# Strassen's algorithm with seven products for the two FFN matrix products behind a linear-attention block

## The chip, the core and the metric

The kernel runs on one core of a Trainium2 chip. The metric is the device time of one execution in microseconds (us). PE is TensorE (matrix products), PEld its weight loads, DVE is VectorE, ACT is ScalarE, POOL is GpSimd, and SP is the queue that starts transfers. SBUF is the on-chip memory and PSUM holds the matrix products' sums. The kernel before takes 1322.14 us, the median of 3 runs (1321.06 to 1322.49).

## The reference

The attention has no softmax: k times v per head, q times that, a division by the root mean square over the 64 columns of a head, and a gain. Its 4,608 by 512 result goes through a gated feed-forward network (FFN). All of it is fp32; the three FFN weights come as 64-bit floats.

```python
kv = np.einsum('bhsd,bhse->bhde', k, v)              # batch 8, heads 8, seq 576, head_dim 64
o = np.einsum('bhsd,bhde->bhse', q, kv)
x = o / np.sqrt(np.mean(o * o, axis=-1, keepdims=True) + 1e-06) * g_norm
x = x.transpose(0, 2, 1, 3).reshape(4608, 512)
g = x @ w_gate                                       # 512 x 1536
val = x @ w_val                                      # 512 x 1536
out = g / (1 + np.exp(-g)) * val @ w_out             # 1536 x 512
```

## The kernel before

The 4,608 tokens are handled in nine blocks of 512. For each block the FFN has 12 "up" units (128 of the 1,536 gate and value columns each) and 4 "down" units (128 tokens each). The attention of the next block is cut into ten steps that stand between these units, so that TensorE never waits for it. Every weight piece is rounded on the chip from 64-bit words to fp32, on VectorE and ScalarE, during block 0.

```python
    class Words:
        def round_to(self, dst):                     # one piece, 128 x 512
            nc.scalar.activation(out=unit, in_=low, func=ACT.Copy, scale=2.0**-51, bias=2.0)
            nc.scalar.activation(out=mag.bitcast(F32), in_=high.bitcast(F32), func=ACT.Abs)
            nc.vector.tensor_scalar(out=mag..., op0=OP.max, op1=OP.min)
            nc.vector.tensor_scalar(out=sign, in0=high, ..., op0=OP.bitwise_and)
            nc.vector.scalar_tensor_tensor(out=mag, in0=mag, scalar=3, in1=sign, ...)
            nc.vector.tensor_tensor(out=dst.bitcast(U32), in0=mag..., in1=unit..., op=OP.add)

    # ... attention: kv, turn_q, product, rms, scale ...

    class Ffn:
        def up(self, j):
            g = g_psum.tile([P, BLK], F32, name="g")
            u = v_psum.tile([P, BLK], F32, name="u")
            for ps, w in ((g, wg), (u, wv)):
                for s in range(NS):                  # 4 steps of 128 along d_model
                    nc.tensor.matmul(ps, lhsT=w[:, s, P * j : P * (j + 1)], rhs=self.x[:, s, :], ...)
            silu = silu_pool.tile([P, BLK], F32, name="silu")
            nc.scalar.activation(out=silu, in_=g, func=ACT.Silu)
            nc.vector.tensor_tensor(out=self.h[:, j, :], in0=silu, in1=u, op=OP.mult)

        def down(self, t):
            ps = o_psum.tile([P, DM], F32, name="ops")
            for j in range(NF):                      # 12 steps of 128 along d_ff
                nc.tensor.matmul(ps, lhsT=self.h[:, j, P * t : P * (t + 1)], rhs=wo[:, j, :], ...)
            nc.scalar.copy(out=o, in_=ps)
            # ... store ...

    pieces = [("g", 0), ("v", 0), ("g", 1), ("v", 1)]
    for j in range(NF):
        pieces += [("g", j + 2), ("v", j + 2)] if j + 2 < NF else []
        pieces += [("o", j)]
```

Of the kernel before, what the change touches and what calls it, by code (L numbers as in the profile page):

```python
# [14 lines left out]
P = 128  # L15
# [3 lines left out]
def kernel(  # L19
# [17 lines left out]



    nc = tc.nc  # L40

    B, H, S, D = q.shape
# [1 line left out]
    FF = moe_w_gate.shape[1]  # L44
    T = 4
    BLK = P * T
    NB = NT // BLK
    NS = DM // P
    NF = FF // P
    KP = 96  # L50
    KT = S // KP
    eps = 1e-6
    assert NT == B * S and NT == NB * BLK and NB == B + 1 and S - BLK == BLK // B
    assert 2 * D == P and H == 2 * NS and KP * KT == S

    def pool(name, bufs, **kw):
        return ctx.enter_context(tc.tile_pool(name=name, bufs=bufs, **kw))

    consts = pool("consts", 1)
    ld_pool = pool("ld", 10)  # L60
    cv_pool = pool("cv", 2)
    qt_pool = pool("qt", 1)
    sq_pool = pool("sq", NS)
    st_pool = pool("st", 1)
    x_pool = pool("x", 2)
    h_pool = pool("h", 1)
    silu_pool = pool("silu", 2)
    o_pool = pool("o", 2)

    PS = bass.MemoryType.PSUM  # L70
    g_psum = pool("g_psum", 2, space=PS)
    v_psum = pool("v_psum", 2, space=PS)
    o_psum = pool("o_psum", 2, space=PS)
    a_psum = pool("a_psum", 2, space=PS)

    ident = consts.tile([P, P], F32, name="ident")
    make_identity(nc, ident)
# [16 lines left out]
    wg = consts.tile([P, NS, FF], F32, name="wg")  # L94
    wv = consts.tile([P, NS, FF], F32, name="wv")
    wo = consts.tile([P, NF, DM], F32, name="wo")

    class Words:

# [17 lines left out]
        def round_to(self, dst):  # L117
            halves = self.raw.rearrange("p (f w) -> p f w", w=2)
            low, high = halves[:, :, 0], halves[:, :, 1]

            unit = cv_pool.tile([P, BLK], F32, name="unit")
            nc.scalar.activation(out=unit, in_=low, func=ACT.Copy, scale=2.0**-51, bias=2.0)  # L122
            mag = cv_pool.tile([P, BLK], U32, name="mag")
            nc.scalar.activation(out=mag.bitcast(F32), in_=high.bitcast(F32), func=ACT.Abs)  # L124
            nc.vector.tensor_scalar(  # L125
                out=mag.bitcast(F32), in0=mag.bitcast(F32), scalar1=self.LOW, scalar2=self.HIGH,
                op0=OP.max, op1=OP.min,
            )
            sign = cv_pool.tile([P, BLK], U32, name="sign")
            nc.vector.tensor_scalar(out=sign, in0=high, scalar1=0x80000000, scalar2=None, op0=OP.bitwise_and)  # L130
            nc.vector.scalar_tensor_tensor(  # L131
                out=mag, in0=mag, scalar=3, in1=sign, op0=OP.logical_shift_left, op1=OP.bitwise_xor
            )
            a, b = self.shape[0], BLK // self.shape[0]
            nc.vector.tensor_tensor(  # L135
                out=dst.bitcast(U32),
                in0=mag.rearrange("p (a b) -> p a b", a=a, b=b),
                in1=unit.bitcast(U32).rearrange("p (a b) -> p a b", a=a, b=b),
                op=OP.add,
            )  # L140
# [14 lines left out]

    def round_w(name, j):
        dst = wviews[name][0]
        words.pop((name, j)).round_to(dst[:, j : j + 1, :] if name == "o" else dst[:, :, P * j : P * (j + 1)])

    class Att:  # L160

# [29 lines left out]
        def kv(self, js):  # L191
            if self.n == B:
                return
            if js[0] == 0:
                self.kv_ps = a_psum.tile([P, NS, D], F32, name="a")
            for j in js:
                for u in range(2):
                    rows = slice(u * D, (u + 1) * D)
                    for c in range(KT):
                        nc.tensor.matmul(  # L200
                            self.kv_ps[rows, j, :], lhsT=self.k[j][:, u, c, :], rhs=self.v[j][:, u, c, :],
                            start=(c == 0), stop=(c == KT - 1),
                        )
            if js[-1] == NS - 1:
                dst, ps = kvs[self.n % 3], self.kv_ps
                nc.scalar.copy(out=dst[0:D, :, 0:D], in_=ps[0:D])
                nc.vector.tensor_copy(out=dst[D:P, :, D:P], in_=ps[D:P])

        def turn_q(self, js):
            if js[0] == 0:  # L210
                self.qt = qt_pool.tile([P, NS, T, P], F32, name="qt")
            for j in js:
                ps = a_psum.tile([P, T, P], F32, name="a")
                hs = slice(2 * (j % 2), 2 * (j % 2) + 2)
                for t in range(T):
                    nc.tensor.transpose(ps[:, t, :], self.q[j // 2][:, t, hs, :], ident)  # L216
                nc.vector.tensor_copy(out=self.qt[:, j], in_=ps)

        def product(self, js):
            n, cut = self.n, self.cut  # L220
            if js[0] == 0:
                self.x = x_pool.tile([P, NS, BLK], F32, name="x")
                self.sq = []
            for j in js:
                ps = a_psum.tile([P, T, P], F32, name="a")
                for b, p0, p1 in ((n - 1, 0, cut), (n, cut, P)):
                    if p1 > p0:
                        nc.tensor.matmul(  # L228
# [4 lines left out]
                sq = sq_pool.tile([P, BLK], F32, name="sq")  # L233
                nc.scalar.activation(out=sq, in_=ps, func=ACT.Square)  # L234
                nc.vector.tensor_copy(out=self.x[:, j, :], in_=ps)  # L235
                self.sq.append(sq)

        def rms(self):


            ps = a_psum.tile([P, BLK], F32, name="a")
            for j in range(NS):
                nc.tensor.matmul(  # L243
                    ps[0:H, :], lhsT=head_of[:, j, :], rhs=self.sq[j], start=(j == 0), stop=(j == NS - 1)
                )
            z = st_pool.tile([H, BLK], F32, name="z")
            nc.vector.tensor_scalar(
                out=z, in0=ps[0:H, :], scalar1=1.0 / D, scalar2=eps, op0=OP.mult, op1=OP.add
            )
            y = st_pool.tile([H, BLK], F32, name="y")  # L250
            nc.vector.tensor_scalar(
# [9 lines left out]

        def scale(self, js):
            for j in js:
                ps = a_psum.tile([P, BLK], F32, name="a")
                nc.tensor.matmul(ps, lhsT=gain[:, j, :], rhs=self.y, start=True, stop=True)  # L265
                nc.vector.tensor_tensor(out=self.x[:, j, :], in0=self.x[:, j, :], in1=ps, op=OP.mult)  # L266

        def steps(self):
            lo, hi = (0, 1), (2, 3)
            return [  # L270
                lambda: self.kv(lo), lambda: self.kv(hi), lambda: self.turn_q(lo), lambda: self.turn_q(hi),
                lambda: self.product(lo), lambda: self.product(hi), self.rms, lambda: None,
                lambda: self.scale(lo), lambda: self.scale(hi),
            ]

    class Ffn:
        def __init__(self, n, x):
            self.n, self.x = n, x
            self.h = h_pool.tile([P, NF, BLK], F32, name="h")

        def up(self, j):
            g = g_psum.tile([P, BLK], F32, name="g")
            u = v_psum.tile([P, BLK], F32, name="u")
            for ps, w in ((g, wg), (u, wv)):
                for s in range(NS):
                    nc.tensor.matmul(  # L286
                        ps, lhsT=w[:, s, P * j : P * (j + 1)], rhs=self.x[:, s, :],
                        start=(s == 0), stop=(s == NS - 1),
                    )
            silu = silu_pool.tile([P, BLK], F32, name="silu")  # L290
            nc.scalar.activation(out=silu, in_=g, func=ACT.Silu)  # L291
            nc.vector.tensor_tensor(out=self.h[:, j, :], in0=silu, in1=u, op=OP.mult)  # L292

        def down(self, t):
            ps = o_psum.tile([P, DM], F32, name="ops")
            for j in range(NF):
                nc.tensor.matmul(  # L297
                    ps, lhsT=self.h[:, j, P * t : P * (t + 1)], rhs=wo[:, j, :],
                    start=(j == 0), stop=(j == NF - 1),
                )  # L300
            o = o_pool.tile([P, DM], F32, name="o")
            nc.scalar.copy(out=o, in_=ps)  # L302
            rows = out[BLK * self.n : BLK * (self.n + 1), :].rearrange("(p t) d -> p t d", t=T)
            nc.sync.dma_start(out=rows[:, t, :], in_=o)


    pieces = [("g", 0), ("v", 0), ("g", 1), ("v", 1)]
    for j in range(NF):
        pieces += [("g", j + 2), ("v", j + 2)] if j + 2 < NF else []
        pieces += [("o", j)]  # L310
    loaded = rounded = 0

    def weights(upto):
# [8 lines left out]
    blocks = [Att(n) for n in range(NB)]  # L322
    blocks[0].load()
    weights(4)
    for step in blocks[0].steps():
        step()

    START = 4
    for n in range(NB):
        ffn = Ffn(n, blocks[n].x)  # L330
        steps = blocks[n + 1].steps() if n + 1 < NB else []
        for unit in range(NF + T):
            if n == 0:
                weights(4 + 3 * (unit + 1))
                if unit == 1:
                    blocks[1].load()
            if unit < NF:
                ffn.up(unit)
            else:
                ffn.down(unit - NF)  # L340
            if 0 <= unit - START < len(steps):
                steps[unit - START]()
            if unit == NF and n + 2 < NB:
                blocks[n + 2].load()


# [29 lines left out]
```

## Time and profile before

| what | value | where it is read |
|---|---|---|
| time | 1322.14 us | median of 3 runs |
| span of the profiled execution | 1315.4 us | head of the page |
| TensorE, VectorE, ScalarE, GpSimd busy | 98, 21, 12, 0% | engine shares |
| FFN starts; block 0 ends | 52.4; 198.75 us | time axis; chain |
| a steady block (FFN and the next block's attention) | 141.95 us | chain |
| the last block (FFN alone) | 123.6 us | chain |

A page gives busy times of the engines, then the span in 40 slices with the busy share of each engine in tenths, then the chain of work that ended last, then groups of instructions. In a group, "c<-xs,ts" names the written tile and the tiles read, "x432" is the count, then come the sum in us, the mean of one in ns, and behind the last bar the idle time of that engine just before these instructions with what ended it. The prediction shows such lines of the kernel before and reads them. One caution for later: the profiled execution of before was a short one (1317.16 us, with a span of 1315.4). In the later sessions its time and its span differ by 1.8 us (1321.52 against 1319.7), so a typical span is near 1,320. Differences of less than 5 us against this one profile are not to be read closely.

### The profile page before, as it was taken

How to read it: one execution, taken by the hardware profiler on the slowest of the kernel's cores; microseconds unless marked ns; L12 is line 12 of the kernel's file. 1: busy time of each engine (PE TensorE's matmuls, PEld its weight loads, DVE VectorE, ACT ScalarE, POOL GpSimd, SP SyncE). 2: the span in 40 equal slices, each digit the busy share in tenths (PEclk: the TensorE clock that was granted, in tenths of full speed). 3: DMA queues.
4: the chain of work that ended last, by engine and by line, in shares of the span. 5: the costliest groups of instructions: out<-in, count | busy, mean ns of one | idle time of the engine just before them, and what ended most of it. 6: DMA issues, size and time to landing. Idle time of an engine off the chain costs nothing.

```text
span 1315.4 us, 9105 instructions
## 1 busy us (share of the span) xinstructions
PE 1286.2 (98%) x3776; PEld 584.8 (44%) x3776; DVE 281.9 (21%) x477; ACT 155.7 (12%) x262; POOL 6.1 (0%) x17
## 2 busy tenths in 40 slices
PE   5699999999999999999999999999999999999998
PEld 3254444544454444544454445444454444444443
DVE  5659500130012200230013001230123002300000
ACT  3236101010001000100101000100010001000000
POOL 1000000000000000000000000000000000000000
PEclk8799999999999999999999999999999999999999
DMA  9267100300021001200030002100100000000000
GB/s 308 61 222 253 44 24 8 93 12 16 16 73 32 9 24 36 69 8 16 8 103 2 16 16 74 32 15 18 32 0 8 16 8 0 0 24 9 0 8 25
DMA packets 72105, 57.22 MB, mean 44 GB/s; under 512 B 41344, under 2 KB 65920, under 8 KB 72064
## 3 DMA queue, kind: packets, MB, share of 16 engines
q1 hardware_dynamic: 71808, 56.64, 14.2%
q8 instruction: 30, 0.49, 0.2%
q14 instruction: 11, 0.09, 0.0%
q0 software_dynamic: 256, 0.00, 0.0%
HBM read 47.19 MB, written 9.44 MB: 43 GB/s over the span
## 4 chain that ended last, share of the span: by engine, by line
PE 91%; DVE 0%; ACT 0%; issue 0%; ACTq 0%; DVEq 0%
PE ops L297 28%; PE g L286 27%; PE u L286 26%; PE a L265 2%; PE a L200 2%; PE a L228 2%; PE a L243 2%; PE a L216 1%; DVE wg L135 0%; DVE mag L131 0%; DVE wo L135 0%; ACT o L302 0%; DVE mag L125 0%; DVE sign L130 0%; ACTq L302 0%
## 5 line engine op out<-in xcount | busy, mean ns | idle before, releaser
L286 PE MATMUL g<-x,wg 128*128 128x512 f32 x864 | 393.9, 598 | 0.3
L286 PE MATMUL u<-x,wv 128*128 128x512 f32 x864 | 388.8, 592 | 0.0
L297 PE MATMUL ops<-wo,h 128*128 128x512 f32 x864 | 377.3, 594 | 0.3 <-DVE wo L135 0.3
L286 PEld LDWEIGHTS u<-x,wv 128*128 128x128 f32 x864 | 164.1, 190 | 207.0 <-issue 204.5
L297 PEld LDWEIGHTS ops<-wo,h 128*128 128x128 f32 x864 | 162.5, 190 | 210.4 <-issue 209.2
L286 PEld LDWEIGHTS g<-x,wg 128*128 128x128 f32 x864 | 161.4, 191 | 197.1 <-issue 189.9
L292 DVE TENSOR_TENSOR h<-silu,u 128x512 f32<-128x512 f32 x108 | 74.1, 686 | 734.4 <-PE u L286 649.4
L291 ACT ACTIVATE silu<-g 128x512 f32<-128x512 f32 x108 | 64.4, 596 | 600.3 <-PE g L286 600.3
L302 ACT COPY o<-ops 128x512 f32<-128x512 f32 x36 | 21.1, 586 | 409.5 <-PE ops L297 409.5
L266 DVE TENSOR_TENSOR x<-x,a 128x512 f32<-128x512 f32 x36 | 24.8, 688 | 171.8 <-PE a L265 171.8
L265 PE MATMUL a<-y,gain 8*128 8x512 f32 x72 | 38.8, 664 | 10.8 <-issue 10.8
L200 PE MATMUL a<-ld 96*64 96x64 f32 x768 | 42.3, 234 | 5.5 <-DMA ld<-in_v_dram 5.5
L200 PEld LDWEIGHTS a<-ld 96*64 96x64 f32 x768 | 40.3, 145 | 15.5 <-issue 15.5
L228 PE MATMUL a<-qt,kv 128*128 128x512 f32 (+7 forms) x128 | 36.2, 422 | 6.1 <-DVE x L235 5.5
L243 PE MATMUL a<-sq,head_of 128*8 128x512 f32 x72 | 33.9, 616 | 0.0
L228 PEld LDWEIGHTS a<-qt,kv 128*128 128x128 f32 x128 | 22.1, 192 | 22.2 <-issue 11.0
L234 ACT ACTIVATE sq<-a 128x512 f32<-128x512 f32 x36 | 21.5, 596 | 60.5 <-PE a L228 60.4
L265 PEld LDWEIGHTS a<-y,gain 8*128 8x128 f32 x72 | 13.0, 198 | 34.9 <-issue 27.5
L122 ACT ACTIVATE unit<-ld 128x512 f32<-128x512 uint32 x36 | 24.6, 682 | 29.9 <-issue 18.4
L235 DVE COPY x<-a 128x512 f32<-128x512 f32 x36 | 24.9, 691 | 14.2 <-ACT sq L234 14.2
L131 DVE SCALAR_TENSOR_TENSOR mag<-mag,sign 128x512 uint32<-128x512 uint32 x36 | 24.6, 684 | 0.1
L124 ACT ACTIVATE mag<-ld 128x512 f32<-128x512 f32 x36 | 24.1, 669 | 0.0
(29 smaller groups left out, 201.1 us busy)
## 6 DMA issues: line engine op xcount, KB each, us to landing
ld<-in_k_dram SPq DMA_DIRECT2D x32, 288.0 KB, 3.9
ld<-in_v_dram SPq DMA_DIRECT2D x32, 288.0 KB, 4.4
out_dram<-o SPq DMA_DIRECT2D x36, 256.0 KB, 2.5
ld<-in_moe_w_gate_dram SPq DMA_DIRECT2D x12, 512.0 KB, 8.1
ld<-in_moe_w_val_dram SPq DMA_DIRECT2D x12, 512.0 KB, 8.1
ld<-in_moe_w_out_dram SPq DMA_DIRECT2D x12, 512.0 KB, 7.7
ld<-in_q_dram SPq DMA_DIRECT2D x16, 128.0 KB, 3.4
ld<-in_q_dram SPq DMA_DIRECT2D x16, 112.0 KB, 2.5
```

The source lines that it names most:

```text
L122: nc.scalar.activation(out=unit, in_=low, func=ACT.Copy, scale=2.0**-51, bias=2.0)
L131: nc.vector.scalar_tensor_tensor(out=mag, in0=mag, scalar=3, in1=sign, op0=OP.logical_shift_left, op1=OP.bitwise_xor)
L200: nc.tensor.matmul(self.kv_ps[rows, j, :], lhsT=self.k[j][:, u, c, :], rhs=self.v[j][:, u, c, :], start=(c == 0), stop=(c == KT - 1),)
L228: nc.tensor.matmul(ps[:, :, p0:p1], lhsT=kvs[b % 3][:, j, :], rhs=self.qt[:, j, :, p0:p1], start=True, stop=True,)
L235: nc.vector.tensor_copy(out=self.x[:, j, :], in_=ps)
L243: nc.tensor.matmul(ps[0:H, :], lhsT=head_of[:, j, :], rhs=self.sq[j], start=(j == 0), stop=(j == NS - 1))
L265: nc.tensor.matmul(ps, lhsT=gain[:, j, :], rhs=self.y, start=True, stop=True)
L266: nc.vector.tensor_tensor(out=self.x[:, j, :], in0=self.x[:, j, :], in1=ps, op=OP.mult)
L286: nc.tensor.matmul(ps, lhsT=w[:, s, P * j : P * (j + 1)], rhs=self.x[:, s, :], start=(s == 0), stop=(s == NS - 1),)
L291: nc.scalar.activation(out=silu, in_=g, func=ACT.Silu)
L292: nc.vector.tensor_tensor(out=self.h[:, j, :], in0=silu, in1=u, op=OP.mult)
L297: nc.tensor.matmul(ps, lhsT=self.h[:, j, P * t : P * (t + 1)], rhs=wo[:, j, :], start=(j == 0), stop=(j == NF - 1),)
```

## The change

The intent is to spend fewer multiplications on the engine that is full. Each FFN product is seen as a 2 by 2 product of blocks, and the Winograd form of Strassen's algorithm needs seven block products in place of eight. TensorE then does 7/8 of the work, in instructions of 256 columns in place of 512. The price is sums before and after: on the tokens (s1 to s4), on the weights (t1 to t4), and on the products. Here p6+p7+p4 and p5+p3 are accumulated in PSUM (banks "b" and "c") and read between the products by VectorE.

For the up stage a11, a12 / a21, a22 are the 256-token halves by the halves of d_model, and b is gate beside value. The t2 sum is made in place in wv (and in wo) while the weights are rounded. For t1, t3 and t4 GpSimd makes differences anew in every block (tiles "ts" in the up stage, "t" in the down stage). Two up units of 128 columns are worked on together, product by product; this is called an up pair here, and a block has six. GpSimd also multiplies silu(g) by u into h, and VectorE makes s1, s3, s2 (and s4) of h for the down stage.

```diff
+    add = lambda e, o, a, b: e.tensor_tensor(out=o, in0=a, in1=b, op=OP.add)      # likewise sub, mul
     def round_w(name, j):
         ...
+        if name == "v":
+            t2 = wv[:, 0:2, fs]
+            sub(nc.vector, t2, wv[:, 2:4, fs], t2)
+            add(nc.vector, t2, t2, wg[:, 0:2, fs])
+        elif name == "o" and j % 2:
+            ...                                    # the same on wo
+    ORDER = (1, 5, 6, 2, 7, 4, 3)
+    CHAIN = {1: ("a", True), 2: ("a", False), 6: ("b", True), 7: ("b", False), 4: ("b", False),
+             5: ("c", True), 3: ("c", False)}
+    # pairs: 1 b11 a11, 2 b21 a12, 3 b22 s4, 4 t4 a22, 5 t1 s1, 6 t2 s2, 7 t3 s3
+    def after1: s = copy of bank a (ScalarE)          def after6: u2 = b + s (VectorE)
+    def after2: g1 = silu(a) (ScalarE)                def after7: u3 = b + s; u3 = c + u3 (VectorE)
+    def after4: g2 = b + s (VectorE), silu (ScalarE); h2 = g2 * u3 (GpSimd)
+    def after3: u2 = c + u2 (VectorE); h1 = g1 * u2 (GpSimd)
     class Ffn:
-        ... up and down of before ...
+        def up(self, j):
+            sub(nc.gpsimd, ts[:, 0], wv[:, 2:4, fs], t2)
+            for i in range(2):
+                sub(nc.gpsimd, ts[:, 1 + i], wg[:, 2 * i : 2 * i + 2, fs], t2)
+            units = [Up(2 * j + e, self.att, ts, e, self.h) for e in range(2)]
+            for p in ORDER:
+                for u in units:
+                    u.multiply(p)
+            add(nc.vector, self.s1[:, j], a21, a22)          # a.. are quarters of h here
+            sub(nc.vector, self.s3[:, j], a21, a11)
+            sub(nc.vector, a21, self.s1[:, j], a11)
+        def down(self, steps): ...                           # two units, seven products of six steps
-    pieces = [("g", 0), ("v", 0), ("g", 1), ("v", 1)] ...    # an output piece after each up pair
+    pieces = [(x, j) for j in range(NF) for x in "gv"] + [("o", j) for j in range(NF)]
```

The lines with "after" are put in one line each here. The rest of the diff is pools (five load buffers in place of ten, one x tile in place of two), and the attention's later steps moved into the down stage.

## The prediction

> **What bounds the kernel now.** I read the page first, then the groups of instructions by form, then the chain that ended last, then single stretches on the time axis. From the page, the busy shares, the slices and the first line of the chain:
>
> ```profile
> PE 1286.2 (98%) x3776; PEld 584.8 (44%) x3776; DVE 281.9 (21%) x477; ACT 155.7 (12%) x262; POOL 6.1 (0%) x17
> ...
> PE   5699999999999999999999999999999999999998
> ...
> DVE  5659500130012200230013001230123002300000
> ...
> PE 91%; DVE 0%; ACT 0%; issue 0%; ACTq 0%; DVEq 0%
> ```
>
> TensorE is busy from the third slice on and carries the chain. VectorE is crowded only in the first five slices (some 165 us), where the weights are turned from 64-bit words into fp32; after that it is nearly idle, and GpSimd does nothing. The groups by form:
>
> ```profile
> L286 PE MATMUL g<-x,wg 128*128 128x512 f32 x864 | 393.9, 598 | 0.3
> L286 PE MATMUL u<-x,wv 128*128 128x512 f32 x864 | 388.8, 592 | 0.0
> L297 PE MATMUL ops<-wo,h 128*128 128x512 f32 x864 | 377.3, 594 | 0.3 <-DVE wo L135 0.3
> L292 DVE TENSOR_TENSOR h<-silu,u 128x512 f32<-128x512 f32 x108 | 74.1, 686 | 734.4 <-PE u L286 649.4
> L131 DVE SCALAR_TENSOR_TENSOR mag<-mag,sign 128x512 uint32<-128x512 uint32 x36 | 24.6, 684 | 0.1
> L125 DVE TENSOR_SCALAR mag<-mag 128x512 f32<-128x512 f32 x36 | 15.2, 422 | 2.8 <-ACT mag L124 2.5
> L207 DVE COPY kv<-a 64x256 f32<-64x256 f32 x8 | 3.4, 427 | 33.1 <-ACT kv L206 33.1
> ```
>
> Each fp32 product is two instructions, so 2,592 of them are the feed-forward network (FFN). The mean of 598 ns includes the pipeline's drain; the spacing of starts is what counts. The time axis has both widths side by side, because the attention product of one block happens to split into columns 256 and 256:
>
> ```profile
> 551.26 1.89 PE L228 MATMUL a<-qt,kv 128*128 128x256 f32 x8
> 552.98 3.60 PE L286 MATMUL g<-x,wg 128*128 128x512 f32 x8
> 556.42 3.60 PE L286 MATMUL u<-x,wv 128*128 128x512 f32 x8
> ```
>
> Eight instructions of 256 columns take 552.98 - 551.26 = 1.72 us, 215 ns each; eight of 512 take 3.44 us, 430 ns each. Halving the width halves the time, although each instruction has a weight load of its own (190 ns, mean of the load groups), which therefore hides even behind 215 ns. A steady block, between the ends of two "down" stages in the chain, is 141.95 us: 288 x 0.4292 = 123.6 us of FFN and 18.3 us of attention for the next block. The last block, FFN alone, takes 123.62 us.
>
> **What the Trainium skill says.** "TensorE: Matmul & The Clock Gate", section Back-to-back issue gap, gives 262 cycles for N=256 and 518 for N=512, so six cycles of overhead either way. An fp32 instruction here streams its columns twice; 512/2.4 + 2.5 = 216 ns and 1024/2.4 + 2.5 = 429 ns fit the trace. "VectorE: DVE Perf Modes", section on the TRN2 errata, gives an fp32 tensor_tensor (N+151)/0.96 ns: 691 at 512 against 686 here, and 424 at 256 (a copy of 256 takes 427 here). "GPSIMD Engine Reference", section 3.1, measures a 2,048-element fp32 add at 4,497 ns, 2.2 ns an element; the trace has no such instruction. "SBUF — State Buffer", section Who interferes with whom, says that a VectorE instruction with two SBUF inputs, or in a two-port mode, and a GpSimd instruction that reads SBUF block each other whole. The trace can't show that, since GpSimd is idle.
>
> **The change part by part.** TensorE: per block an "up" of 12 column tiles x 7 products x 2 steps and a "down" of 2 x 7 x 6, together 252 products or 504 instructions, of 256 columns. The instruction listing of both programs confirms 9 x 252 products against 1,296. 504 x 0.2158 = 108.8 us in place of 123.6: a gain of 14.8 us a block, 133.6 us in all. This is the full eighth, and all on the path. Attention stays at 18.3 us, so a steady block is 127.1 us if nothing else waits.
>
> VectorE, steady block: 60 adds that read PSUM in the up and 10 in the down, 18 sums of h, all of 256 elements at 0.42 us, are 37 us; s4 is 1,536 elements, about 1.75 us; four sums of x at 0.69 are 2.7; the attention's work (copies, the chain for 1/rms, scaling) is 16. Sum 57 us of 127. ScalarE stays below that: about 50 instructions of 256 at 0.37 us, plus four squares. GpSimd, as an estimate at the skill's 2.2 ns: 18 differences of 512 (1.17 us), 24 products of 256 (0.62), three of 1,536 (3.4): 46 us. So no engine comes near to TensorE's load; only latency can cost time there.
>
> Where it can, I followed the order of both programs. In an up stage each engine passes through the seven products of two units, 0.86 us per product and unit. The tight place is product 4, which needs the bank that the sum u3 has just read: about 0.16 us of drain, 0.42 for the add and some 0.1 for signals, against 0.86 us of the other unit's product. It fits with 0.15 us to spare. At the entry to the down stage GpSimd's queue holds a 3.4 us difference of wo in front of the last h products, so product 1 waits perhaps 1 us. In the down stage s4 stands on VectorE ahead of a copy that frees the only other "m" bank (the sum of squares now holds one of the two): 0.7 us, or 4 us if GpSimd's 3.4 us difference, released by the same product, gets the port first. The rms chain, about 8.2 us, has 8.6 us of products over it. I charge 3.5 us a block.
>
> Start-up is where I expect to pay. Before, the FFN begins at 52.4 us and block 0 ends at 198.75. Now, ahead of the first products, VectorE has rounding for eight to ten weight pieces, the sums on wv and the sums of x: about 43 us of instructions from 15.3 us on, so the FFN starts near 58. Then until the ups of block 0 end: 28 pieces at four operations (0.34 + 0.34 + 0.60 + 0.60 = 1.9 us start to start, as VectorE's row on the time axis shows in back-to-back stretches) less what was begun, 50 us; sums on wv and wo, 10; 78 adds at 0.34, 26. That is 86 us, to 144, against 72.6 us of products. GpSimd's estimated 39 us in that time contend with about 66 us of it; if all of it excludes, the ups end at 183; I take 168. What is left for TensorE then, most of the down and most of block 1's attention, is about 50 us, plus some waits for loads through five buffers instead of ten. Block 0 ends at about 220, with 205 to 242 possible: 21 us later than before, 36 us later than its own products would allow.
>
> Sum: 220 + six blocks of 127.1 + a block without keys and values (before 136.7, so 122) + the last block 108.8 + 8 x 3.5 + 4 us of final store = 1,245 us of span. The runs are about 7 us longer than the profiled span (1,322.1 against 1,315.4): 1,252 us. I round to 1,250.
>
> **Rivals.** (a) The full eighth: start-up no later than 195 and no waits, 1,315 - 134 + 5, about 1,190 us. For it speaks that no engine is near full later; against it that VectorE is at nine tenths of slices 80 to 140 us already before, and gets some 35 us more there. (b) Contention and queue order bind each up: if every VectorE instruction with two SBUF inputs waits for a GpSimd one, the last sum of h in each pair slips by 2 to 3 us and delays the adds that free bank b; 1 us in each of 54 ups and 4 us in each down is 85 us, and the time 1,305 us, "same". Against it: 5 us lie between those sums and the next urgent add. (c) Narrow instructions stream no faster than the weight loads: at 240 ns instead of 216 the FFN costs 110 us more, no gain. The eight at 215 ns speak against it, though a sustained stream of them was never seen.
>
> **Range and chances.** Start-up between 205 and 242 and waits of 1 to 8 us a block give about 1,218 to 1,293. Faster by over 2% means below 1,296: 0.92. Within 2% needs (b) or (c): 0.07. Slower: 0.01.
>
> **What would show it.** Right: the groups of 128x256 products, 4,536 instructions, start 216 ns apart; a steady block at 129 to 133 us, with VectorE near 45% and GpSimd near 35%; block 0 ends near 220 with TensorE waiting for VectorE in slices 2 to 5. Wrong: weight loads with no gap between them (c); waits of products on VectorE or GpSimd in every up (b); GpSimd's 512-element difference well over 1.2 us, or VectorE's sums of h and s4 stretched beyond 0.42 and 1.75 us, which would be the port.

## The result, and the profile after

The changed kernel is correct and takes 1300.62 us, the median of 4 runs (1300.58 to 1302.02), against 1321.6 us for the kernel before in the same session. The ratio is 0.9844 (95% interval 0.9827 to 0.9862). Ratios here are the mean time of one kernel's fast runs over that of the other's of the same rounds, so they are not quite the ratio of the medians. This is less than 2% faster, and outside the predicted range.

The page of the changed kernel: busy times, three rows of slices, and the first line of the chain.

```profile
PE 1198.3 (92%) x5720; PEld 957.6 (74%) x5720; DVE 682.4 (53%) x1242; ACT 212.2 (16%) x478; POOL 480.9 (37%) x422
...
PE   6587779999999999999999999999999998999898
...
DVE  3978885545444545544545454446354634553441
...
POOL 1134431354325532454244434433443235423541
...
PE 76%; DVE 11%; POOL 10%; DMA 1%; issue 1%; ACT 1%; SPq 0%; POOLq 0%; DVEq 0%; ACTq 0%
```

TensorE was 98% busy and had 91% of the chain. Now it has 76% of the chain, and VectorE and GpSimd have 21% between them, although neither is near full after the first six slices. In those slices (195 us) TensorE is at 5 to 8 tenths, where before it was at 9 from the third slice on. The groups by form of the changed kernel that matter below:

```profile
L337 PE MATMUL a<-x,wg 128*128 128x256 f32 x864 | 212.8, 389 | 16.2 <-DVE wg L158 16.2
L119 POOL TENSOR_TENSOR h<-g,u 128x256 f32<-128x256 f32 x216 | 162.9, 771 | 45.8 <-ACT g L382 42.8 <-DVE u L117 3.0
L118 POOL TENSOR_TENSOR ts<-wg,wv 128x512 f32<-128x512 f32 x108 | 140.3, 1307 | 0.0
L337 PE MATMUL c<-xs,ts 128*128 128x256 f32 x432 | 111.8, 396 | 32.9 <-DVE u L117 31.8 <-POOL ts L118 0.7
L117 DVE TENSOR_TENSOR u<-b,s 128x256 f32<-128x256 f32 x252 | 106.1, 423 | 211.0 <-PE b L337 210.4
L117 DVE TENSOR_TENSOR s<-h 128x256 f32<-128x256 f32 x54 | 67.2, 1244 | 136.4 <-POOL h L119 136.4
```

Three things stand out. Product 5 (bank c from xs and ts) is the product that waits, 31.8 us in all, for VectorE's sum "u". The add with one PSUM operand takes 423 ns as foreseen. The first sum of h, which has two SBUF operands and the same size, takes 1,244 ns. Now a stretch of the chain in the middle of block 2 (columns: start us, length us, what):

```profile
387.34 3.47 PE b L337 x16
...
390.94 1.27 POOL ts L118
392.21 0.68 POOL h L119
392.89 1.23 POOL ts L118
394.12 0.70 POOL h L119
...
394.84 1.47 DVE s L117
396.31 0.34 DVE u L117
...
396.69 1.13 PE c L337 x4
```

The first line gives sixteen narrow instructions in 3.47 us, 217 ns each: the narrow products run as fast as predicted, with 504 weight loads a block beside them. The rest is one release chain. The first line ends with product 4, which releases a buffer of weight differences, so GpSimd starts the next three (1.27 us each). It alternates them with the products that make h. VectorE's first sum of h waits for the second of those, takes 1.47 us, and only behind it comes the add "u" (0.34 us of the chain, 0.41 on the time axis) that frees bank c for product 5 of the second unit. The add's own data had long been there, since TensorE had finished that product at about 392.4. TensorE has bridged part of this with products that didn't need the bank, and stands still for 1.59 us; with the restart, a pair with such a wait takes 13.94 us in place of 12.09, 1.85 us more. The trace has 20 such waits, two in each of blocks 1 to 6 and four in each of blocks 7 and 8, and 20 x 1.59 is the 31.8 us above.

In the source the three sums of h stand behind both units' adds. In the trace the first sum runs ahead of the second add, so the queue of the built program isn't in the source's order. And the sum itself is stretched: it takes 1.47 us beside a difference on GpSimd, where sums of its size take 0.42 undisturbed. By these two numbers some 1.05 of the 1.59 us is stretch, as an estimate; no run keeps this order and takes the stretch alone away.

Where the time went, by the ends of the down stages. "Own products" is the block before less 14.85 us (123.6 - 108.75).

| stretch | before | own products | after | lost |
|---|---|---|---|---|
| up to the end of block 0 | 198.75 | 183.9 | 247.3 | 63.4 |
| each of blocks 1 to 6 | 141.95 | 127.1 | 132.9 | 5.8 |
| block 7 (no keys and values left to do) | 136.7 | 121.85 | 131.4 | 9.6 |
| block 8 (FFN alone) | 123.6 | 108.75 | 118.3 | 9.5 |

That makes 63.4 + 35 + 9.6 + 9.5 = 117.5 us, and 133.6 less this is the gain of 16 us that the two spans show (1315.4 - 1298.9). Half of the loss is start-up; half recurs block by block.

For start-up, two stretches of VectorE and TensorE in the changed kernel (length, then PE, PEld, DVE, ACT and POOL busy with counts, then granted clock, DMA share and GB/s):

```profile
100.00:120.00 20.00, 15.53 (x56) 12.03 (x56) 17.07 (x34) 7.63 (x15) 8.19 (x7) 0.84 0.36 107
160.00:180.00 20.00, 13.92 (x71) 10.46 (x69) 19.97 (x47) 10.15 (x16) 0.00 (x0) 0.91 0.49 156
```

VectorE is the fullest engine in both. In the second, where the twelve output pieces are rounded in a row, it has no gap. In block 0 the starts of product 3 in the six up pairs are 19.5, 19.8, 19.5, 22.2 and 28.5 us apart, where TensorE needs 12.1. Some VectorE instructions in block 0 are also far longer than their size. From the time axis of the changed kernel, GpSimd and VectorE together:

```profile
189.67 3.61 POOL L118 TENSOR_TENSOR t<-wo 128x1536 f32<-128x1536 f32 x1
190.02 3.54 DVE L118 TENSOR_TENSOR h<-s,h 128x256 f32<-128x256 f32 x1
...
199.16 3.43 POOL L118 TENSOR_TENSOR t<-wo 128x1536 f32<-128x1536 f32 x1 [5.88 <-PE c L337]
199.46 4.75 DVE L118 TENSOR_TENSOR s<-h 128x1536 f32<-128x1536 f32 x1 [4.54 <-PE c L337]
```

A sum of 256 elements, usually 0.42 us, takes 3.54 us and ends 0.28 us after GpSimd's difference. The 1,536-element sum takes 4.75 us, where it takes 1.76 without such a neighbour (below). This is the mutual exclusion that the prediction quoted and could not see in the kernel before.

Standing still is only part of the loss in block 0. TensorE's gaps there add up to 32.8 us, and its first FFN product comes 4 us later than before; for the rest of the 63.4 us it is busy, but partly slower. Its row on the time axis in the third pair:

```profile
100.48 2.07 PE L337 MATMUL a<-x,wg 128*128 128x256 f32 x4 [4.05 <-DVE wg L158]
103.55 3.30 PE L337 MATMUL c<-xs,ts 128*128 128x256 f32 x8
107.12 1.89 PE L337 MATMUL a<-x,wg 128*128 128x256 f32 x8
```

After a standstill of 4.05 us eight narrow instructions take 3.30 us, and the next eight 1.89. The granted clock was 0.50 between 100.4 and 103.5 us and 1.00 between 107 and 115. In the ups of block 0 about 50 narrow instructions start 0.4 us after the one before in place of 0.22, some 10 us in all. No experiment tells how much of this lengthened block 0 and how much fell in time that VectorE needed anyway.

### The profile page after: what moved, and what is told of

Read it like the earlier page. It is cut to its first block, busy times and chain, and to the rows that moved or that the text cites. A ratio compares the mean times of both kernels' runs of the same rounds, so it can differ in the third digit from the quotient of the medians.

```text
span 1298.9 us, 14910 instructions
## 1 busy us (share of the span) xinstructions
PE 1198.3 (92%) x5720; PEld 957.6 (74%) x5720; DVE 682.4 (53%) x1242; ACT 212.2 (16%) x478; POOL 480.9 (37%) x422
## 4 chain that ended last, share of the span: by engine, by line
PE 76%; DVE 11%; POOL 10%; DMA 1%; issue 1%; ACT 1%; SPq 0%; POOLq 0%; DVEq 0%; ACTq 0%
PE b L337 31%; PE a L337 17%; PE c L337 17%; POOL ts L118 4%; POOL h L119 4%; PE m L232 3%; PE m L260 3%; PE m L294 3%; DVE s L117 3%; PE m L268 3%; POOL t L118 2%; DVE mag L154 1%; DVE u L117 1%; DMA ld<-in_v_dram 1%; PE m L248 1%
## 5 line engine op out<-in xcount | busy, mean ns | idle before, releaser
L337 PE MATMUL a<-x,wg 128*128 128x256 f32 x864 | 212.8, 389 | 16.2 <-DVE wg L158 16.2
L117 DVE TENSOR_TENSOR u<-b,s 128x256 f32<-128x256 f32 x252 | 106.1, 423 | 211.0 <-PE b L337 210.4
L337 PEld LDWEIGHTS a<-x,wg 128*128 128x128 f32 x864 | 165.4, 194 | 43.6 <-DVE wg L158 17.8
L118 POOL TENSOR_TENSOR t<-wo 128x1536 f32<-128x1536 f32 x27 | 105.6, 3910 | 235.4 <-PE b L337 114.8
L119 POOL TENSOR_TENSOR h<-g,u 128x256 f32<-128x256 f32 x216 | 162.9, 771 | 45.8 <-ACT g L382 42.8
L337 PE MATMUL c<-xs,ts 128*128 128x256 f32 x432 | 111.8, 396 | 32.9 <-DVE u L117 31.8
L118 POOL TENSOR_TENSOR ts<-wg,wv 128x512 f32<-128x512 f32 x108 | 140.3, 1307 | 0.0
L117 DVE TENSOR_TENSOR s<-h 128x256 f32<-128x256 f32 x54 | 67.2, 1244 | 136.4 <-POOL h L119 136.4
L337 PEld LDWEIGHTS c<-xs,ts 128*128 128x128 f32 x432 | 83.0, 197 | 54.8 <-DVE u L117 39.8
L337 PE MATMUL b<-x,ts 128*128 128x256 f32 x432 | 105.5, 385 | 3.1 <-DVE u L117 3.0
L337 PE MATMUL b<-x,wv 128*128 128x256 f32 x432 | 105.6, 385 | 0.0
L337 PE MATMUL c<-xs,wv 128*128 128x256 f32 x432 | 105.0, 384 | 0.0
## 6 DMA issues: line engine op xcount, KB each, us to landing
ld<-in_q_dram SPq DMA_DIRECT2D x16, 128.0 KB, 3.0
```

The lines of the kernel that those rows point to most:

```text
L117: add = lambda e, o, a, b: e.tensor_tensor(out=o, in0=a, in1=b, op=OP.add)
L118: sub = lambda e, o, a, b: e.tensor_tensor(out=o, in0=a, in1=b, op=OP.subtract)
L119: mul = lambda e, o, a, b: e.tensor_tensor(out=o, in0=a, in1=b, op=OP.mult)
L337: nc.tensor.matmul(ps, lhsT=lhsT, rhs=rhs, start=first and i == 0, stop=i == self.steps - 1, skip_group_check=True,)
```

## The experiments

Two theories stood for the loss in every block. **Order**: the add that frees bank c stands behind sums of h that nobody needs soon. **Port**: VectorE and GpSimd exclude each other, and the stretched sums delay everything. The two can act together, as the 1.47 us sum above shows. For start-up the suspects were the same exclusion, the added in-place sums on the weights, the order of the pieces, and plain throughput of VectorE. All kernels start from the changed one. "Block 0" below is the end of its down stage, "steady" the period of blocks 1 to 6, "last" block 8 alone, all from the traces.

| kernel | time (us) | ratio to before, 95% interval | block 0 | steady | last | result |
|---|---|---|---|---|---|---|
| changed kernel | 1300.62 | 0.9844 (0.9827 to 0.9862) | 247.3 | 132.9 | 118.3 | correct |
| e1_sums_last | 1262.77 | 0.9564 (0.9547 to 0.9581) | 249.8 | 129.2 | 110.8 | correct |
| e2_pool_h_first | 1255.71 | 0.9501 (0.9485 to 0.9517) | 250.1 | 128.0 | 108.8 | correct |
| e3_no_pool_reads | 1235.9 | 0.9359 (0.9345 to 0.9373) | 230.1 | 128.0 | 108.8 | wrong |
| e4_no_weight_sums | 1283.96 | 0.9718 (0.9702 to 0.9735) | 231.1 | 132.9 | 118.3 | wrong |
| e5_both_orders | 1252.59 | 0.9485 (0.9466 to 0.9504) | 248.6 | 128.0 | 108.8 | correct |
| e6_block0_plain | 1209.65 | 0.9165 (0.9152 to 0.9179) | 203.5 | 128.0 | 108.8 | correct |
| e8_neither | 1219.09 | 0.9231 (0.9217 to 0.9245) | 212.9 | 128.0 | 108.8 | wrong |
| e9_pieces_spread | 1251.69 | 0.9474 (0.946 to 0.9488) | 245.3 | 128.0 | 108.8 | correct |
| e10_neither_spread | 1225.34 | 0.927 (0.9255 to 0.9286) | 219.6 | 128.0 | 108.8 | wrong |

### e1_sums_last: VectorE's sums of h behind the urgent add

```diff
     def after3(self):
-            add(nc.vector, self.u2, self.bank("c"), self.u2)
+            self.end = add(nc.vector, self.u2, self.bank("c"), self.u2)
...
-            add(nc.vector, self.s1[:, j], a21, a22)
-            sub(nc.vector, self.s3[:, j], a21, a11)
-            sub(nc.vector, a21, self.s1[:, j], a11)
+            with tc.issue_after(units[1].end.ins):
+                add(nc.vector, self.s1[:, j], a21, a22)
+                sub(nc.vector, self.s3[:, j], a21, a11)
+                sub(nc.vector, a21, self.s1[:, j], a11)
```

> Only one thing moves: on VectorE the three sums of h come after the second unit's last u2 add instead of the first of them standing in front of it. Theory A (the loss in a steady block is this queue order: the sum waits for a GpSimd product of h, the u2 add waits behind it, and TensorE's product 5 waits for the add to free bank c): an up stage without attention work falls from 13.94 to 12.1 us, a steady block from 132.9 to about 127.5, the last block from 118.3 to about 109, the run from 1300.6 to about 1251 us; block 0 still ends near 247. Rival B (the shared SBUF port stretches VectorE's sums, whatever the order): ups stay above 13.4 us and the run above 1290.

Not one operation fewer, and GpSimd's differences are untouched, yet the time falls by 38 us. An up pair without attention work falls from 13.94 to 12.09 us, which is what its products need. The first sum of h still takes 1.25 us on average, so behind the add the stretch costs nothing. The expected 1251 us was missed by 12: a steady block keeps a wait of 1.2 us at the entry of the down stage and the last block one of about 2 us, and block 0 ends 2.5 us later. The chain of this kernel at that entry:

```profile
456.17 3.44 POOL t L118
459.61 2.06 POOL h L119 x3
...
461.71 3.29 PE a L337 x14
```

GpSimd's difference of wo for the down stage stands ahead of the last three products of h, and product 1 of the down stage waits for these.

### e2_pool_h_first: GpSimd's differences behind the products of h

```diff
+    muls = []
+    def behind(k):
+        return tc.issue_after(muls[-k]) if len(muls) >= k else nullcontext()
...
-            sub(nc.gpsimd, ts[:, 0], wv[:, 2:4, fs], t2)
-            for i in range(2):
-                sub(nc.gpsimd, ts[:, 1 + i], wg[:, 2 * i : 2 * i + 2, fs], t2)
+            with behind(2):
+                sub(nc.gpsimd, ts[:, 0], wv[:, 2:4, fs], t2)
+                for i in range(2):
+                    sub(nc.gpsimd, ts[:, 1 + i], wg[:, 2 * i : 2 * i + 2, fs], t2)
...
-            sub(nc.gpsimd, t, of, t2)
+            with behind(2 if p == 5 else 1):
+                sub(nc.gpsimd, t, of, t2)
```

> GpSimd makes the four products of h of a pair before any difference of weights; VectorE's order is as good as unchanged (a sum of h still stands in front of the second u2 add). Theory A': the products of h are late only because two 1.3 us differences stand between them, so the first sum of h is ready 2.5 us earlier and bank c is free in time: up 12.1 us, steady block about 126 to 127.5 since the wait of 1 to 2 us at the entry of the down stage goes too, run about 1240 to 1252. Rival (port contention alone): as the differences then run beside other VectorE sums, the wait only moves: up above 13, run above 1285.

The time falls by 45 us, and both waits are gone: a steady block takes 128.0 us and the last one 108.8, which is 504 instructions of 215.8 ns. The time is 4 us above the expected 1240 to 1252, and a steady block 0.5 above its range; block 0, here too, ends 2.8 us later than in the changed kernel. The same stretch of the chain, at the entry of the down stage, is TensorE alone:

```profile
455.21 1.73 PE c L337 x8
456.94 0.87 PE m L248 x8
457.81 5.18 PE a L337 x24
```

So the wait can be broken at either end: the products of h come earlier, or the add doesn't stand behind them. Here the first two sums of h stand ahead of the second unit's add:

```profile
389.60 0.42 DVE L117 TENSOR_TENSOR u<-c,u 128x256 f32<-128x256 f32 x1 [0.44 <-PE c L337]
390.45 0.93 DVE L117 TENSOR_TENSOR s<-h 128x256 f32<-128x256 f32 x1 [0.43 <-POOL h L119]
391.30 0.41 DVE L118 TENSOR_TENSOR s<-h 128x256 f32<-128x256 f32 x1
391.64 0.41 DVE L117 TENSOR_TENSOR u<-c,u 128x256 f32<-128x256 f32 x1
```

But the first one starts earlier, 0.85 us after the first unit's add (389.60 to 390.45), where in the changed kernel it was 3.15 us (391.69 to 394.84), and it takes 0.93 us in place of 1.47. So e2 shortens both the sum's wait and its stretch, and doesn't part them.

### e3_no_pool_reads: GpSimd no longer reads SBUF for the differences

```diff
-            sub(nc.gpsimd, ts[:, 0], wv[:, 2:4, fs], t2)
-            for i in range(2):
-                sub(nc.gpsimd, ts[:, 1 + i], wg[:, 2 * i : 2 * i + 2, fs], t2)
+            nc.gpsimd.memset(ts, 0.01)
...
-            sub(nc.gpsimd, t, of, t2)
+            nc.gpsimd.memset(t, 0.01)
```

The result is wrong (relative error 54.8).

> Wrong results on purpose: GpSimd fills the tiles of weight differences with a constant instead of computing them, so it reads SBUF only for the products of h, and its queue is shorter. If the shared port stretches VectorE's instructions with two SBUF inputs: the first sum of h falls from a mean of 1.24 us to below 0.6, the s4 difference from 2.09 to about 1.7, the rounding's 1.4 us instructions in start-up go back to 0.42 and 0.69, and block 0 ends 10 to 25 us earlier than 247. Steady block about 127. Run about 1215 to 1240. If the port does not matter: durations stay, block 0 ends within 4 us of 247.

Steady and last block are those of e2, and block 0 ends 17.2 us earlier than in the changed kernel. Three groups of this kernel, of which the first two show the stretching gone:

```profile
L154 DVE SCALAR_TENSOR_TENSOR mag<-mag,sign 128x512 uint32<-128x512 uint32 x36 | 24.5, 680 | 0.1
L118 DVE TENSOR_TENSOR h<-s,h 128x256 f32<-128x256 f32 x54 | 22.6, 419 | 1.2
L117 DVE TENSOR_TENSOR s<-h 128x256 f32<-128x256 f32 x54 | 50.3, 932 | 37.7 <-POOL h L119 37.7
```

The rounding step falls from a mean of 774 to 680 ns, the longest third sum of h from 3.54 to 0.43 us. That s4 then takes 1.76 us shows what it costs undisturbed. One expectation failed: the first sum of h was to fall below 0.6 us and still takes 0.93, and GpSimd's products of h, which still read SBUF, run beside it. For the steady blocks this run is no test of the port alone, because the order changed with it: here both units' adds (381.62 and 382.49 us) run ahead of the first sum (383.62). The 17.2 us contain, besides the exclusion, the differences' own time and their wait for the rounded weights; this run doesn't part these.

### e4_no_weight_sums: the in-place t2 sums left out

```diff
-        if name == "v":
-            ...                                        # two sums of 256 on wv
-        elif name == "o" and j % 2:
-            ...                                        # two sums of 256 on wo
```

The result is wrong (relative error 2.2).

> Wrong results on purpose: the 36 in-place sums on the gate/value and output weights are left out of the rounding, about 15 us of VectorE work between 20 and 181 us. If VectorE's throughput bounds start-up, block 0 ends 10 to 16 us earlier, at 231 to 237, and the run takes about 1287; if loads, GpSimd or the attention of block 1 bound it, less than 4 us. A steady block stays at 132.9.

Block 0 ends 16.2 us earlier; nothing else moves. The 36 instructions are 36 x 0.42 = 15 us of VectorE if undisturbed; 8 of them start before the FFN does. The prediction's 10 us stood for those behind the FFN's start alone. Practically all of the 15 us is on the path.

### e5_both_orders: e1 and e2 together

The edits of e1 and e2 in one kernel.

> Both changes of order together: GpSimd makes the products of h before the differences, and VectorE makes the sums of h after the second u2 add. If the two orders cure one and the same wait, the second adds nothing to the first: steady block 128.0 us, last block 108.8, run within 3 us of the 1255.7 of the GpSimd order alone. If there are two waits in an up stage, another 3 us or more per steady block go.

The time is 1252.59 us, 3 us below e2, and their intervals overlap. The periods are those of e2. In this kernel, though, sums of h run beside GpSimd's work, the second beside a product of h and the third beside a difference. From its time axis in block 1:

```profile
261.69 0.94 DVE L118 TENSOR_TENSOR s<-h 128x256 f32<-128x256 f32 x1
262.66 1.37 DVE L118 TENSOR_TENSOR h<-s,h 128x256 f32<-128x256 f32 x1
```

These two sums would take 0.42 us each undisturbed, and still a steady block is 128.0 us as in e2. So stretched sums cost nothing there as long as no urgent add stands behind them. In the steady blocks mending the order is enough; that exclusion had no part in the changed kernel's wait is not shown.

### e6_block0_plain: block 0 in the form of before

Block 0 is computed with 512-column products as before, with the old order of pieces; the t2 sums go to GpSimd behind the last use of the plain weights; blocks 1 to 8 are those of e5. Cut to its core:

```diff
-        if name == "v": ... elif name == "o" and j % 2: ...       # sums on VectorE, in round_w
+    def sum_wv(j):
+        sub(nc.gpsimd, t2, wv[:, 2:4, fs], t2)
+        add(nc.gpsimd, t2, t2, wg[:, 0:2, fs])
+    def sum_wo(j): ...                                            # the same on wo, during block 1
+    class Plain: ...                                              # up and down of the kernel before
+    for f in range(NF):
+        weights(4 + 3 * (f + 1) if f < 8 else len(pieces))
+        plain.up(f)
+    for j in range(NP):
+        sum_wv(j)
...
-    for n in range(NB):
+    for n in range(1, NB):
```

> Block 0 in the old form (512-column products, no sums, weight pieces in the old order), the in-place weight sums made by GpSimd between the stages that read the old and the new contents, blocks 1 to 8 in the new form with both orders mended. If start-up's loss comes from doing the new form while the weights are still being rounded on VectorE: block 0 ends at 199 to 204 us as before the change, the later blocks take 128.0 and 108.8, and the run about 1204 to 1212 us, 8 to 9% below before. If start-up's loss comes from the smaller load pool and the later attention of block 1, block 0 ends at 220 or later.

The result is correct, and at 1209.65 us this is the fastest of all kernels here, 8.35% under before. Block 1 starts at 203.5 us. The load pool of five and the attention in the down stage are as in the changed kernel, and block 1 starts only 4.75 us later than before the change; so beside plain products these two cost no more than that. Beside the new form they were not tested alone. TensorE's row of slices in this kernel:

```profile
PE   6599999999999999999999999999999999999998
```

It is full from the third slice on, as in the kernel before.

### e8_neither: e3 and e4 together

The edits of e3 and e4 in one kernel, wrong (relative error 26.5).

> Wrong results on purpose: neither differences on GpSimd nor in-place weight sums on VectorE. Each alone ended block 0 at 230 and 231 instead of 247. If the two are separate charges on VectorE, block 0 ends near 214 (run about 1219); if they are the same slack seen twice, not before 226. What remains above 184, the old start-up less block 0's own gain, is then the 78 adds of the new form and the order of the work.

Block 0 ends at 212.9 us, 34.4 earlier than in the changed kernel; 17.2 + 16.2 = 33.4, so the two charges add up. What remains is 212.9 - 183.9 = 29 us. In this kernel VectorE is busy for 87.7 us from 58 us to the end of the ups at 163.4. TensorE's gaps in block 0 add up to 14 us.

### e9_pieces_spread and e10_neither_spread: the old order of the weight pieces

```diff
-    pieces = [(x, j) for j in range(NF) for x in "gv"] + [("o", j) for j in range(NF)]
+    pieces = [("g", 0), ("v", 0), ("g", 1), ("v", 1)]
+    for j in range(NF):
+        pieces += [("g", j + 2), ("v", j + 2)] if j + 2 < NF else []
+        pieces += [("o", j)]
...
-                weights(4 * (j + 2))
+                weights(4 + 6 * (j + 1))
```

This edit is made once on e5 and once on e8.

> Both orders of e5_both_orders, and besides the weight pieces in the order of the kernel before: an output-weight piece after each pair of up pieces, six pieces per up, in place of four per up and the 12 output-weight pieces all in the last up of block 0. Correct result expected. In the changed kernel the last up of block 0 takes 28 us instead of about 20 because those pieces are rounded there. If the bunching is itself a cause of the late start-up (VectorE waits early for TensorE and is overfull later), block 0 ends 5 to 15 us earlier than the 248.6 us of e5_both_orders, and the time falls from 1252.6 to 1238 to 1248 us. Rival: VectorE's total throughput sets the start-up, wherever the pieces stand: block 0 ends within 3 us of 248.6 and the time is 1250 to 1256 us; the earlier ups of block 0 then take 22 to 24 us instead of 20.

> The kernel of e8_neither (no GpSimd reads for the differences, no weight sums; wrong result on purpose, the same as there) with the weight pieces spread as in e9_pieces_spread. In e8_neither five ups of block 0 take about 15.5 us each, where TensorE needs 12.1, the last one 31 us, and block 0 ends at 212.9, 29 us later than its products allow. If the bunched output-weight pieces are what is left of the loss there, block 0 ends near 200, 10 to 15 us earlier, and the time is 1204 to 1210 us. Rival, VectorE's throughput: the ups take 18 us each instead, block 0 ends at 210 to 214 as before, and the time stays within 1215 to 1222 us.

On e5, block 0 ends 3.3 us earlier and the time is the same within the intervals. The early up pairs take 24 to 27 us in place of e5's 19 to 22, and the last takes 13 in place of 29. On e8 it ends 6.7 us later, at 219.6, which neither the expectation (near 200) nor its rival (210 to 214) had; why it is later was not found. So the idea that bunching the twelve output pieces is itself a cause falls; the work of VectorE in block 0 moves along with the pieces.

## Why the prediction was wrong

The sign was right, and so was the mechanism of the gain; 1,250 us was 50.6 us too low, and the range's upper end was more than 7 us too low. That end doesn't follow from its own terms: block 0 at 242 and waits of 8 us add 22 and 36 us to 1,252, which is 1,310, so "Within 2% needs (b) or (c)" doesn't follow either. Its sum of the span was 1,245 us against 1,298.9. Of these 54 us, block 0 is 27.3 us (247.3 against 220), six steady blocks 6 x 2.3 = 14, block 7 is 5.9 (131.4 against 122 + 3.5), and the last 6.0 (118.3 against 108.8 + 3.5). Adding 7 us from span to run was also wrong: the difference is 1.7 us here, which hid some 5 us of the miss.

**Right.** The narrow instructions run at 216 ns beside a weight load each, in a sustained stream: rival (c) is refuted by the last block of 108.8 us in e2. TensorE's gain of 14.8 us a block is there in full in the last block of e2, e3, e5 and e6, and 13.95 us of it in a steady block (141.95 to 128.0). The 3.4 us difference ahead of the last products of h costs 1.2 us at the entry to a steady block's down stage, where "perhaps 1 us" was said. VectorE's adds with a PSUM operand cost 0.42 us. A steady block of 129 to 133 us was named, and 132.9 is at its edge, with some luck: most of the 5.8 us is a wait that the 3.5 us didn't hold. Two of the signs of being wrong that it named came true, waits of products on VectorE in ups (though not in every one) and stretched sums of h. GpSimd is 37% busy against 35 named; VectorE at 53% was put at 45.

**Wrong: "Against it: 5 us lie between those sums and the next urgent add."** This is the step that failed in the steady blocks. The text had looked for the tight place at product 4 and bank b. The 5 us hold for the source's order, in which the sums follow both adds. It overlooked that in the built program the second unit's sum of u2, which frees bank c, is queued on VectorE behind the first sum of h, and that this sum waits for GpSimd and is stretched by it. The bank is wanted 2.6 us after its last product (two first products and the first unit's product 5, at 0.86 each), and comes 1.6 to 1.9 us too late. Rival (b) was put too low with it. Its effect, waits in the ups, is what happened, and e1 and e2 show that mending the queue's order takes it away. But its size was 1.85 us in 20 of the 54 pairs, not 1 us in each pair and 4 in each down stage (a sum that gives 90 us, not the 85 written). The last block shows it bare: four such waits, 4 x 1.85 = 7.4 of its 9.5 us, which is the 7.5 us that e1 takes away; the other 2 us are the wait at the entry of the down stage, which e2 takes away.

**Wrong: "That is 86 us, to 144, against 72.6 us of products", then "I take 168" and "Block 0 ends at about 220".** From 60 to 190 us VectorE was busy for 106.7 us, not 86. The ups ended near 188 and block 0 at 247.3, beyond the 242 called possible. Its three terms, one by one. The sums on wv and wo cost 16.2 us (e4); at the prediction's 0.34 us all 36 would be 12, so this was some 4 us short. Making the differences costs 17.2 us of end time (e3), and it must be added in full, as e8 shows; the 24 us between 144 and 168 were meant for it, so this term alone was not too small. The third is the assumption that the rest, VectorE's busy time, fits without gaps until 144. Without either charge, in e8, the ups should then have ended at 134 (58 + 86 - 10) and ended at 163.4: VectorE was busy for 87.7 us in place of 76 and idle for the other 17.7. Block 0 ended 29 us after its products would allow. With e6 (same pools, same attention order, at 203.5) and with e9 and e10 (order of pieces) it is likely that these 29 us belong to the new form's own work in block 0, its adds on VectorE between the pieces and their chain with GpSimd and TensorE, TensorE's slower stretches after its standstills among it. This is by elimination: no run took those adds away one by one, and the cause of the 29 us stays open in so far. Also "What is left for TensorE then ... is about 50 us" was 59.

**Where the expected gain went**, then: of the 133.6 us, about 63 are lost at start-up; leaving block 0 in the plain form, without its 14.85 us of saved products, gives 44 of them back. About 54 are lost in blocks 1 to 8, and e5 gives back 48 us by the order of two queues, without taking an operation away. Open stay the split of the 17.2 us of e3, the split of the steady blocks' wait between order and stretch, and the 0.9 us by which a steady block of e2 is longer than 127.1.

## What to carry to other kernels

When an engine's work is cut, follow each buffer of the new form from its last reader back through that reader's queue, and ask what stands in the queue ahead of it: an add of 0.4 us cost 38 us here because a sum nobody needed soon was queued before it. Read that queue's order from the trace, since it was not the source's here. Average busy shares of 53 and 37% said nothing of this. A form that trades TensorE work for VectorE work belongs in the stages where VectorE is idle, and a stage where it is already full (here the block in which weights are rounded) is better left in the old form.

## What the Trainium skill lacked or had wrong

- "SBUF — State Buffer", Who interferes with whom: the runs agree, and give durations for such a pair, of which that section has only ratios: a 0.42 us sum took 3.54 us beside a 3.61 us difference on GpSimd, and one of 1.76 us took 4.75.
- "GPSIMD Engine Reference", section 3.1, has one size for an add of two tensors, 4,497 ns at 2,048 elements. The runs have 0.73 us at 256, 1.27 at 512 and 3.43 at 1,536 where nothing disturbs, about 2.11 ns an element and 0.19 us fixed, which gives 4.51 us at 2,048. The prediction, at 2.2 ns an element, wrote 0.62, 1.17 and 3.4; 2.2 ns alone gives 0.56, 1.13 and 3.38.
- "TensorE: Matmul & The Clock Gate", Back-to-back issue gap, calls its formula that of an isolated product, with sustained spacing set by the weight loads as well. For fp32 it fits sustained streams: 504 narrow instructions, each with a load of 190 ns, take 108.8 us, 215.8 ns each.
- No page that I read has an example of a small instruction that frees a PSUM bank from behind a waiting one in an in-order queue; it cost 1.85 us here in 20 of 54 up pairs.
